# Nine due times of routing matmuls moved in a three-part kernel (linear attention, gated layer, eight routed experts)

## The chip, the cores and the metric

The kernel runs on one core of one Trainium2 chip. The metric is the device time of one execution in microseconds, on the slowest (here the only) core. TensorE is called PE below, VectorE DVE, ScalarE ACT, GpSimd POOL; SP issues DMAs.

## The reference, cut to what matters

Three stages stand one behind the other, on 3072 tokens of width 512. The third is the one that the change touches:

```python
x = linear attention with decay (4 x 8 heads, 768 steps, head size 64)   # -> 3072 x 512
h = x @ w_in;  g = h * tanh(softplus(h));  x = g @ w_out                 # 512 -> 2048 -> 512

def _moe2_ref(x, w_gate, w1, w2):            # E = 8 experts, 1024 wide
    cap = N // E                             # 384 tokens for each expert
    logits = x @ w_gate
    order = np.argsort(-logits.flatten())    # best (token, expert) pairs first
    for idx in order:
        tok, e = idx // E, idx % E
        if assigned[tok] >= 0 or counts[e] >= cap: continue
        assigned[tok] = e; counts[e] += 1
    for e in range(E):
        mask = assigned == e
        out[mask] = np.maximum(x[mask] @ w1[e], 0.0) @ w2[e]
```

Each expert gets exactly 384 tokens.

## The kernel before

All large products are made of three half-precision ones (high by high, high by low, low by high), so each operand is split in a high and a low part. Attention and the gated layer fill the span up to about 780 us. The experts follow one another on PE from 801 us to the end. An expert runs over 8 blocks of its hidden width (12 products of 128x384 each) and then over 3 blocks of its 384 tokens (24 products of 128x512 each), 168 products in all. They are recorded at line 526 in the helper `mm3`, which pauses after every 4 products. Their results go to PSUM buffers `ph` and `px` in turn; ACT (lines 922, 923, 940) and DVE (line 924) empty these.

**Routing** (`route_round`, round r fills one expert) runs beside this, mostly on DVE. A round finds the threshold score of the expert that fills first, by five base-64 digits. For digit i there is a compare on DVE (`against`, line 695, into tile `ld`; the first digit's compare is the largest), then a count on PE (`pc`, 24 small products, line 743), a test on DVE (745), and an answer product on PE (`pn`, line 748) that DVE reads back (750, 754). They are named by round: `pc4x0x` is the first count of round 4 and `pn4x9x` its last answer. After the last answer DVE marks the chosen tokens (lines 759 to 770), PE makes two products for their positions (`pp`, lines 789 and 790), and DVE takes the chosen ones out of the score table `L` (792, 794), from which the next round starts (705 to 726, then the compare of its first digit). `route_list` makes a round's list of token numbers: compares on DVE in three groups into tile `amt` (line 695), 24 small products on PE (`pl`, line 823), and the list is read at 826 and 828. It is needed for gathering the tokens of that expert, on POOL's queue.

**Weights** (`weights`): for each expert the two weight matrices are loaded by an indirect DMA on POOL's queue (line 866) once the round has named the expert (`EWI`, line 777), squared and summed on ACT (line 872, four pieces each), totalled on PE (`pt`, line 186), and split into `WIN` or `WOUT` by ACT (229) and DVE (230), four pieces each. Experts with even r use `WIN`, those with odd r `WOUT`.

**What sets the order.** PE and, in this part, ACT run in the order in which the program issues their work; a scheduler orders DVE and POOL. The order is written by the planner `Weave`: it has a clock `now`, which the main line moves by 0.163 (128x384) or 0.216 (128x512) for each product, in pauses of 4 (the constant `pw`); a side step is put into the order at the first pause at or after its due time, and names the wait until its next step (and a cost, such as 0.65 at each answer product, that moves the clock). So a larger wait in this table does not make an engine sleep: it puts the product further behind in PE's order, behind more expert products, and all later steps of the same chain with it. The waits of the routing come from `KN['rs'][r]`: entries 0, 2, 4, 6, 8 are added to the wait ahead of the five counts, entries 1 to 9 (odd) ahead of the five answers, entry 10 ahead of the `pp` products, entry 11 ahead of the list's `pl` products. Two more rules bind the chains: a list is begun only after the `pp` of its round, and round r only after the list of round r-2. `weights` for expert r waits for the round's last answer to be in the order.

Of the kernel before, what the change touches and what calls it, by code (L numbers as in the profile page):

```python
# [20 lines left out]
B, H, S, D = 4, 8, 768, 64  # L21
DM, DFF, E, F = 512, 2048, 8, 1024
# [14 lines left out]
UNIT = [256.0 ** i for i in reversed(range(len(DIGITS)))]  # L37


KN = dict(ea=1, sc=1, pw=4, le=0.0, hl=['P', 'P'], cs=['V', 'V', 'V', 'V', 'V', 'V', 'V'], cc=['V', 'V', 'V', 'V', 'V', 'V', 'V', 'V', 'V'], lo=['c0', 'g', 'c1', 'm', 'c2', 's', 'wg', 'w0', 'w1', 'w2'], ga=['', 'V'], rs=[[-0.63, 0.3, -1.2, 0.0, 0.24, 0.0, 0.09, 0.0, 0.21, 0.0, 0.0, -4.24], [2.1, 0.09, 2.19, 0.0, 0.58, 0.15, 0.18, 0.15, 0.26, 0.26, 1.46, -0.41], [3.26, 0.0, -0.68, 0.2, 0.33, 0.0, -0.3, 0.0, 0.09, -0.12, 0.3, -3.18], [0.56, 0.0, 0.38, 0.0, 0.15, 0.0, 0.12, -0.11, -0.04, -0.27, 0.03, -3.34], [0.67, 0.0, 0.31, -0.76, 0.89, 0.0, 0.15, -0.22, 0.0, 0.0, -0.16, -4.15], [1.46, -2.35, 0.04, -0.29, 0.13, -2.18, 0.42, -0.4, 0.45, 0.03, 1.16, -4.07], [0.45, 0.54, 0.45, 0.0, 1.18, 0.0, -0.39, -0.55, -0.61, -0.05, 0.45, -3.57], [-0.15, 0.0, -0.75, 0.0, 0.0, 0.0, 0.0, -0.3, 0.0, 0.0, 3.28, -3.01]], fs=[[0.0, 0.0, -3.96, -1.22], [-0.75, 0.0, 1.32, 0.16], [0.0, 0.0, -2.08, 0.13], [0.0, -1.13, 0.71, 0.36], [0.0, 0.0, 0.0, -0.56], [0.38, 0.75, 0.13, 0.04], [0.0, 0.38, 0.2, 0.69], [0.0, -1.5, -0.61, 0.29]], av=[5.75, 5.75, 2.0, 4.0], a2=[1.3, 2.2, 4.3], a1=[0.1, 1.0, 0.85], ao=[3.5, 3.5, 3.35], wv=[8.5, 0.5, 1.0, 4.5], ov=5.0, an=[3.0, 3.15, 3.6], qm=['P0', 'VP', 'VP', 'PH', 'P1', 'VV', 'VP'], vm=['P0', 'VP', 'VP', 'VP', 'VP', 'P0', 'VP'], km=['A', 'H', 0, 0, 0, 0, 0], am=['VP', 'VP', 'VP', 'AV', 'VP', 'AV', 'VP'], ss=['V', 'P', 'P', 'P', 'P', 'P', 'P'], sm=['P', 'V', 'V', 'P', 'E', 'D', 'P'], ym=[0, 0, 0], hm=['VVVP', 'VVAV', 'VVVP', 'VVVP', 'AVVP', 'VVVP', 'VVVP', 'VVVP', 'VVVP'], ci=['PP', 'PP', 'AP', 'PP', 'PP', 'PP', 'VP', 'PP'], co=['AP', 'PP', 'PP', 'PP', 'AP', 'PP', 'PP', 'PP'], wa=[15, 12, 8, -1, 7, 16], cp=[0, 100, 0, 100], np=0, yp=[0, 2000], op=[0, 0, 200, 0, 50, 1000], xp=[0, 0, 0, 0, 0, 0], ld=[0, 1, 2, 3, 4], wj=[4, 4, 4], fw=[13.5, 18.5, 14, 16, 14, 16], qs=1.0, tw=3.0, sw=1.5, po=[[0] * 8] * 4, sl=[0, 0, 0.7], rw=[2.6, 2.5, 1.55, 1.7, 1.7], pn=0.5, lw=11.0, gx=9.0, tk=2.75, st=[16.0, 21.0, 20.0, 23.5], wi=['H', 'A', 0, 0, 2, 0, 0, 0], wo=['H', 'H', 0, 0, 0, 0, 'H', 0], tp=[], gw=5.15, nw=1.0, cw=0, sp=50, ap=1000, wp=None, ip=None)  # L40


class Weave:
# [55 lines left out]
def moe_kernel(ctx, tc, qkv, w_in, w_out, w_gate, w1p, w2p,  # L99
# [64 lines left out]
    def first_loads():  # L164
        for x in KN['lo']:
            if x[0] == 'c':
                load_chunk(0, int(x[1]), 3 if x == 'c0' else 1)
            elif x == 'g':
                SY.dma_start(GQ, c_g)
                SY.dma_start(GV, c_gv)  # L170
            elif x == 'm':
                SY.dma_start(MASK, c_mask)
            elif x == 's':
                SY.dma_start(GS, c_gs)
            elif x == 'wg':
                SY.dma_start(wg_raw, w_gate.rearrange("(k p) e -> p k e", p=128))
            else:
                win_load(int(x[1]))


    def col(name, n=1, dt=F32, bufs=2):
        return wk.tile([128, n], dt, name=name, tag=name, bufs=bufs)

    def total(cols, n, tag="tot", name="pm"):
        p = ps.tile([128, 16], F32, name=name, tag="pm", bufs=1)
        T.matmul(p[:, :n], onesf, cols, start=True, stop=True)
        r = col(tag)
        V.tensor_reduce(r, p[:, :n], axis=AX.X, op=OP.add)
        return r

    def pow2(ss, name, bufs=2, n=1):
        a = col(name + "a", n, I32, bufs=bufs)
        V.tensor_scalar(a, ss.bitcast(I32), 1, 0x7F800000, op0=OP.logical_shift_right, op1=OP.bitwise_and)
        r = wk.tile([128, 2, n], I32, name=name, tag=name, bufs=bufs)
        cc = (189 + 16) << 23
        V.tensor_scalar(r[:, 0], a, -1.0, float(cc), op0=OP.mult, op1=OP.add)
        V.tensor_scalar(r[:, 1], a, float((254 << 23) - cc), None, op0=OP.add)
        rf = r.bitcast(F32)
        return rf[:, 0], rf[:, 1]
# [40 lines left out]
    def to_f32(dst, raw, mode='PP'):  # L240

        lo, hi = words(raw)
        di = dst.bitcast(I32)
        hf = hi.bitcast(F32)
        if mode[0] == "A":
            A.activation(dst, hf, AF.Copy, scale=2.0 ** -112)
        else:
            (V if mode[0] == "V" else P).tensor_scalar(dst, hf, 2.0 ** -112, 1.0, op0=OP.mult, op1=OP.mult)
        (V if mode[1] == "V" else P).tensor_scalar(hf, hf, 0.0, 1.0, op0=OP.mult, op1=OP.mult)
        V.scalar_tensor_tensor(di, di, 3, hi, op0=OP.logical_shift_left, op1=OP.bitwise_or)  # L250
        V.scalar_tensor_tensor(di, lo, 29, di, op0=OP.logical_shift_right, op1=OP.bitwise_or)
# [4 lines left out]
    def norm(zs, ss):  # L256

        p = ps_m([128, 128], F32)
        n = len(zs) * 8
        for i, z in enumerate(zs):  # L260
            zb = z.bitcast(BF).rearrange("p (b d two) -> p b d two", d=128, two=2)[:, :, :, 1]
            for b in range(8):
                T.matmul(p, zb[:, b], zb[:, b], start=i + b == 0, stop=8 * i + b == n - 1)
        t = wk.tile([128, 128], F32, name="tr", tag="tr", bufs=1)
        V.tensor_tensor(t, p, identf, op=OP.mult)
        V.tensor_reduce(ss, t, axis=AX.X, op=OP.add)
# [3 lines left out]
    def win_load(i):  # L270
        q, j = divmod(i, 2)
        raw = GF[i % 5 // 3][:, i % 5 % 3 * 2048:i % 5 % 3 * 2048 + 2048]
        SY.dma_start(raw.bitcast(I32).rearrange("p (k f) -> p k f", k=2),
                     w_in_w.rearrange("(k p) f -> p k f", p=128)[:, 2 * j:2 * j + 2, q * 1024:q * 1024 + 1024])
        WIN_RAW.append(raw)
# [3 lines left out]
    def win_setup(q):  # L279

        zs = [RAW[:, i * 1024:i * 1024 + 1024] for i in (2 * q, 2 * q + 1)]
        for j in range(2):
            with tc.high_priority(offset=KN['cp'][q]):
              to_f32(zs[j], WIN_RAW[2 * q + j], KN['ci'][2 * q + j])
            if 2 * q + j < 3:
                win_load(2 * q + j + 5)
        yield KN['wv'][0], 0.0
        yield KN['wv'][1], 1.0
        ss = col("ssi")
        norm(zs, ss)  # L290
        yield KN['wv'][2], 0.2
        sw = pow2(total(ss, 1, "toti"), "swin", 4)
# [925 lines left out]
```

## Time and profile before

| what | value |
|---|---|
| median of 3 runs | 1115.99 us (1115.18 to 1117.84) |
| the profiled execution | 1116.19 us |
| its span, first to last instruction | 1114.3 us |
| PE busy | 972.5 us, 87% of the span |
| DVE busy | 774.0 us, 69% |
| ACT busy | 648.8 us, 58% |
| POOL busy | 417.6 us, 37% |
| mean granted TensorE clock | 0.94 of full speed |

The last 313 us hold the eight experts. The profile names each small product by its round and step, so that each place of the routing can be found in the trace of PE in order of time.

### The profile page before, as it was taken

How to read it: one execution, taken by the hardware profiler on the slowest of the kernel's cores; microseconds unless marked ns; L12 is line 12 of the kernel's file. 1: busy time of each engine (PE TensorE's matmuls, PEld its weight loads, DVE VectorE, ACT ScalarE, POOL GpSimd, SP SyncE). 2: the span in 40 equal slices, each digit the busy share in tenths (PEclk: the TensorE clock that was granted, in tenths of full speed). 3: DMA queues.
4: the chain of work that ended last, by engine and by line, in shares of the span. 5: the costliest groups of instructions: out<-in, count | busy, mean ns of one | idle time of the engine just before them, and what ended most of it. 6: DMA issues, size and time to landing. Idle time of an engine off the chain costs nothing. (4 is left out here: it accounts for less than half of the span.)

```text
span 1114.3 us, 19615 instructions
## 1 busy us (share of the span) xinstructions
PE 972.5 (87%) x7897; PEld 560.0 (50%) x7897; DVE 774.0 (69%) x1630; ACT 648.8 (58%) x989; POOL 417.6 (37%) x304
## 2 busy tenths in 40 slices
PE   3348758888999999999999989999598898899997
PEld 2335434444655555656556546454354454455553
DVE  6899998954666787677776745568779777754530
ACT  4435856554467577577567567316365763767751
POOL 5956365461432553534554513200222222123211
PEclk9959878969999999999999989999699998999999
DMA  8461262157113113121144010053464465266300
GB/s 307 124 189 39 104 179 58 49 104 152 26 52 85 40 57 77 48 76 39 48 105 92 14 38 1 11 194 119 95 218 171 110 193 189 58 218 225 116 29 29
DMA packets 108811, 113.65 MB, mean 102 GB/s; under 512 B 92464, under 2 KB 92592, under 8 KB 106672
## 3 DMA queue, kind: packets, MB, share of 16 engines
q1 hardware_dynamic: 102576, 66.24, 23.0%
q0 software_dynamic: 6144, 46.15, 11.6%
q8 instruction: 62, 1.02, 0.4%
q14 instruction: 29, 0.24, 0.1%
HBM read 77.50 MB, written 13.64 MB: 82 GB/s over the span
## 5 line engine op out<-in xcount | busy, mean ns | idle before, releaser
L526 PE MATMUL ph<-xt,WIN 128*128 128x384 f16 x1728 | 334.8, 336 | 7.5 <-DVE RAW L556 3.2
L526 PE MATMUL px<-WOUT,G 128*128 128x512 f16 x1248 | 312.7, 385 | 0.2 <-DVE WOUT L230 0.2
L526 PEld LDWEIGHTS <-WIN 128*128 128x128 f16 x1920 | 188.6, 101 | 151.9 <-issue 27.4
L526 PEld LDWEIGHTS <-G 128*128 128x128 f16 x1728 | 164.6, 99 | 173.2 <-issue 9.0
L578 POOL TENSOR_TENSOR G<-RAW,G 128x1536 f16<-128x1536 f32 (+1 forms) x32 | 99.5, 3108 | 104.8 <-DVE G L575 88.8
L407 POOL TENSOR_TENSOR amt<-amt 128x512 f16<-128x512 f32 x40 | 55.7, 1393 | 120.7 <-DVE amt L404 106.0
L556 DVE TENSOR_SCALAR RAW<-ph 128x384 f32<-128x384 f32 x124 | 68.1, 551 | 43.1 <-PE ph L526 42.5
L563 ACT ACTIVATE RAW<-RAW,zt,ch 128x1536 f32<-128x1536 f32 x32 | 53.3, 1664 | 49.1 <-DVE RAW L556 44.0
L326 ACT ACTIVATE junk<-ld 128x512 bf16<-128x512 f32 x63 | 39.4, 626 | 61.1 <-DMA ld<-in_qkv_dram 60.2
L924 DVE TENSOR_TENSOR G<-G,G 128x384 f16<-128x384 f32 x64 | 35.4, 554 | 56.3 <-ACT G L923 56.2
L572 DVE TENSOR_TENSOR RAW<-RAW 128x1536 f32<-128x1536 f32 (+1 forms) x33 | 60.7, 1839 | 15.5 <-ACT RAW L571 15.4
L872 ACT ACTIVATE junk<-RAW 128x1024 bf16<-128x1024 f32 x64 | 67.6, 1056 | 5.4 <-DMA RAW<-in_w1p_dram,MASK 2.9
L224 POOL TENSOR_TENSOR RAW<-ld,RAW 128x512 f16<-128x512 f32 x34 | 45.7, 1358 | 50.9 <-ACT RAW L223 49.2
L941 POOL DMA_INDIRECT out_dram<-G,MASK x18 | 23.4, 1300 | 96.3 <-ACT G L940 94.8
L526 PEld LDWEIGHTS <-WOUT 128*128 128x128 f16 x384 | 37.9, 101 | 26.8 <-issue 4.2
L401 DVE TENSOR_TENSOR amt<-pa,MASK 128x512 f32<-128x512 f32 x38 | 26.1, 688 | 35.5 <-PE pa L400 31.1
L571 ACT ACTIVATE RAW<-RAW 128x1536 f32<-128x1536 f32 (+1 forms) x33 | 47.7, 1446 | 0.4
L224 POOL TENSOR_TENSOR STH<-SC,STH 64x256 f16<-64x256 f32 x34 | 32.0, 942 | 42.0 <-ACT STH L223 38.9
L564 ACT ACTIVATE RAW<-RAW 128x1536 f32<-128x1536 f32 x32 | 47.2, 1475 | 0.3
L526 PE MATMUL ph<-WOUT,G 128*128 128x512 f16 x192 | 44.5, 379 | 0.5 <-DVE G L924 0.4
L695 DVE TENSOR_TENSOR ld<-MASK,ld 128x1536 bf16<-128x1536 bf16 (+1 forms) x35 | 44.6, 1274 | 0.5
L526 PE MATMUL px<-WIN,G 128*128 128x512 f16 x192 | 44.1, 380 | 0.0
(571 smaller groups left out, 1946.2 us busy)
## 6 DMA issues: line engine op xcount, KB each, us to landing
ld<-in_qkv_dram SPq DMA_DIRECT2D x20, 768.0 KB, 4.7
G<-in_w_in_dram SPq DMA_DIRECT2D x8, 1024.0 KB, 7.1
G<-in_w_out_dram SPq DMA_DIRECT2D x8, 1024.0 KB, 5.9
x_rows<-xr SPq DMA_DIRECT2D x24, 256.5 KB, 3.1
G<-in_qkv_dram SPq DMA_DIRECT2D x2, 768.0 KB, 6.7
g_columns<-G SPq DMA_DIRECT2D x1, 1024.0 KB, 8.4
G<-g_columns SPq DMA_DIRECT2D x1, 1024.0 KB, 7.3
ld<-in_qkv_dram SPq DMA_DIRECT2D x3, 256.0 KB, 2.9
```

Of the source, the lines that this page charges most:

```text
L224: (V if pool in ("V", "E") else P).tensor_tensor(lo, src, hi, op=OP.subtract)
L326: A.activation(junk(), x.rearrange("p a d -> p (a d)"), AF.Square, accum_out=ss[:, i:i + 1])
L407: (P if mode[1] == "P" else V).tensor_tensor(amh[:, j, 1], am, amh[:, j, 0], op=OP.subtract)
L526: T.matmul(p, a, b, start=i == 0, stop=i == n - 1)
L556: V.tensor_scalar(hs[:, f], p[:, :G], 1.0 / 65536.0, None, op0=OP.mult)
L563: A.activation(th, hs, AF.Tanh, scale=ch[:, q:q + 1], bias=z)
L564: A.activation(th, th, AF.Arctan, scale=-0.5, bias=0.5)
L571: A.activation(th[:, w], th[:, w], AF.Sin, scale=-2.0, bias=math.pi / 2)
L572: (V if hm[1] == 'V' else P).tensor_tensor(th[:, w], th[:, w], hs[:, w], op=OP.mult)
L578: (P if lo == 'P' else V).tensor_tensor(gb[:, 1, o], th[:, w], gb[:, 0, o], op=OP.subtract)
L695: V.tensor_tensor(out.rearrange("p t (j v) -> p t j v", v=VR), cv[:, ts, None, :].to_broadcast([128, n, J // VR, VR]), RT["jr"][:, i, :J]. ...
L872: A.activation(junk(1024), RAW[:, o:o + 1024], AF.Square, accum_out=ss[:, j:j + 1])
```

## The change

Only the table `rs` of the planner's constants differs. No instruction is added or removed; nine waits get other values (rounds count from 0):

```diff
 rs, entry:        first count (0)   positions (10)   list (11)
-round 2                                              -3.18
+round 2                                              -1.68
-round 3                              0.03            -3.34
+round 3                              2.73            -2.54
-round 4            0.67             -0.16
+round 4           -0.53              3.34
-round 5            1.46              1.16            -4.07
+round 5           -1.04              3.66            -2.07
-round 6                              0.45
+round 6                              2.95
```

So the `pp` products of rounds 3, 4, 5 and 6 are due 2.7, 3.5, 2.5 and 2.5 later, the `pl` products of lists 2, 3 and 5 are due 1.5, 0.8 and 2.0 later (counted from the place where their chain stands), and the first counts of rounds 4 and 5 are due 1.2 and 2.5 sooner.

## Rows read from the trace of the kernel before

**Rows 1.** Busy time by expert (1, 2, 3, 7): stretch, length, engines' busy, clock, DMA
```profile
841.46:882.98 41.52, 37.29 (x348) 21.17 (x347) 33.15 (x90) 25.91 (x44) 10.35 (x8) 1.00 0.50 159
882.98:929.59 46.61, 39.80 (x327) 21.98 (x326) 37.41 (x102) 29.80 (x47) 12.08 (x9) 0.92 0.47 142
929.59:977.11 47.52, 40.90 (x324) 21.85 (x323) 34.96 (x95) 25.86 (x43) 9.47 (x10) 0.90 0.46 148
1074.97:1106.27 31.30, 31.30 (x169) 16.35 (x167) 4.46 (x8) 9.05 (x19) 2.91 (x3) 1.00 0.07 26
```

**Rows 2.** PE's waits from 801.3 to 1107 us: waiter, awaited, us, times, longest
```profile
PE pp4x10x L789 <- DVE MASK L765: 3.2, 1, 3.2
PE pp3x10x L789 <- DVE MASK L765: 2.2, 1, 2.2
PE pp5x10x L789 <- DVE MASK L765: 2.1, 1, 2.1
PE pp6x10x L789 <- DVE MASK L765: 2.0, 1, 2.0
PE pc6x0x L743 <- DVE MASK L726: 1.5, 1, 1.5
PE pt5x3x L186 <- DVE se L196: 1.4, 1, 1.4
PE pl2x11x L823 <- DVE amt L695: 1.1, 2, 0.8
...
PE pl5x11x L823 <- DVE amt L695: 1.0, 2, 0.7
...
PE pl5x11x L823 <- DVE GQ L816: 0.8, 1, 0.8
...
PE pc6x8x L743 <- DVE ld L695: 0.8, 1, 0.8
PE pl3x11x L823 <- DVE amt L695: 0.7, 1, 0.7
...
PE pp6x10x L790 <- DVE MASK L770: 0.3, 1, 0.3
```

**Rows 3.** PE in order of time behind `pp` of round 4: start, us, instructions
```profile
889.64 2.73 PE L526 MATMUL ph<-xt,WIN 128*128 128x384 f16 x8
892.17 3.59 PE L526 MATMUL px<-xt,WIN 128*128 128x384 f16 x12
895.59 2.11 PE L526 MATMUL ph<-xt,WIN 128*128 128x384 f16 x12
897.54 2.11 PE L526 MATMUL px<-xt,WIN 128*128 128x384 f16 x12
```

**Rows 4.** PE in order of time behind `pp` of round 5 and behind `pl` of list 5
```profile
928.59 1.21 PE L526 MATMUL px<-WIN,G 128*128 128x512 f16 x4
...
933.08 2.11 PE L526 MATMUL px<-xt,WOUT 128*128 128x384 f16 x12
...
942.12 2.72 PE L526 MATMUL px<-xt,WOUT 128*128 128x384 f16 x8
...
948.10 1.46 PE L526 MATMUL px<-xt,WOUT 128*128 128x384 f16 x8
```

**Rows 5.** DVE in order of time: from `pp` to the next round's first compare
```profile
852.28 0.21 DVE L792 SCALAR_TENSOR_TENSOR MASK<-pp3x10x,MASK 128x48 f32<-128x48 f32 x1
...
854.97 1.75 DVE L695 TENSOR_TENSOR ld<-MASK,ld 128x3072 bf16<-128x3072 bf16 x1
...
890.38 1.28 DVE L230 SCALAR_TENSOR_TENSOR WOUT<-RAW,se,WOUT 128x1024 f16<-128x1024 f32 x1
...
893.89 1.75 DVE L695 TENSOR_TENSOR ld<-MASK,ld 128x3072 bf16<-128x3072 bf16 x1
...
937.57 0.35 DVE L726 TENSOR_TENSOR MASK<-MASK 128x192 bf16<-128x192 f32 x1
```

**Rows 6.** DMA issues from 760 to 1114 us: size or count, median us to landing
```profile
RAW<-in_w1p_dram,MASK POOLq DMA_INDIRECT x7, 9.7
```

## What the change will do: the prediction

> **What bounds the kernel now.** The page gives PE as the busiest engine, and the last 305 us are where the moved products stand. So I cut the last 305 us by expert [rows 1]. Expert 7, which has no routing beside it, takes 31.30 us at full clock, and PE is busy all of it: this is the floor of an expert. Experts 1, 2 and 3 take 41.52, 46.61 and 47.52 us. Part of the excess is the routing's own products, which stay. The rest is PE idle or PE slow: in expert 2 it is busy 39.80 of 46.61 us at a mean granted clock of 0.92, in expert 3 40.90 of 47.52 us at 0.90. DVE is the busiest other engine (37.41 us in expert 2), but it is not full. From 801 us to the end PE runs one fixed order with the same products before and after, so a wait there is paid by everything behind it: the end moves by what PE's waits and slow stretches change.
>
> Then PE's waits, by name [rows 2]. The four longest are the `pp` products of rounds 4, 3, 5 and 6, each for DVE's marking of the chosen tokens: 3.2, 2.2, 2.1 and 2.0 us. After each of them the second `pp` product waits again for the running sum, 0.2 to 0.3 us (four such, the longest is shown). The lists 2, 5 and 3 cost 1.1, 1.0 + 0.8 and 0.7. So these products stand too early in PE's order: PE reaches them and nothing behind them may pass.
>
> Last, what follows a wait. Behind `pp` of round 4 [rows 3] 8 + 12 products take 895.59 - 889.64 = 5.95 us; the next 12 take 897.54 - 895.59 = 1.95, that is 0.1625 each, so 20 should take 3.25. The loss is 2.70: PE was granted the lower of its two clock levels, 1.2 in place of 2.4 GHz. Behind `pp` of round 5 [rows 4] 4 wide and 12 narrow products take 4.49 us instead of 2.8 (a wide one is (31.30 - 96 x 0.1625)/72 = 0.218 by expert 7), a loss of 1.7. Behind list 5 24 narrow products and an answer take 948.10 - 942.12 = 5.98 instead of 3.9 to 4.0, a loss of 2.0. Together 6.4 us of slow clock.
>
> **The change part by part.** The planner's table moves products in PE's order; I added up its due times by hand for both tables (4 expert products move its clock by 0.65 or 0.86, a step lands at the first pause at or after its due time). Number of expert products between two steps, before and after:
>
> - last answer to `pp`: round 3 16 to 32, round 4 12 to 36, round 5 16 to 36, round 6 12 to 32
> - `pp` to the next round's first count: 3 to 4 40 to 32, 4 to 5 44 to 28, 5 to 6 36 to 36
> - first count to list: list 2 4 to 12, list 3 4 to 16, list 5 4 to 20; list 4 stays 44 behind its `pp`
> - from there on the rounds stand later by 8 (round 4), 16 to 20 (round 5), 28 to 36 (round 6) and 52 products (the `pp` of round 7)
> - the w1 loads of experts 4, 5, 6, 7 move 4, 8, 20, 24 products later with their first squares; their w2 loads move by 4 or less
>
> *The `pp` products.* What PE needs between the last answer and `pp` is its work there plus its wait. Round 3: 16 x 0.1625 + 2.2 + 0.2 = 5.0; now it has 32 x 0.1625 = 5.2. Round 4: 12 x 0.1625 + 3.2 + 0.2 = 5.4; now 5.85. Round 5: 2.8 + 2.1 + 0.2 = 5.1; now about 6.1. Round 6: 12 x 0.218 + 2.0 + 0.3 = 4.9; now 5.2 (narrow products stand there then). All four are covered if DVE takes as long as before. Gone: 3.2 + 2.2 + 2.1 + 2.0 + 0.9 = 10.4; what is left of it I bound by 0 and 1.5 and take 0.4.
>
> *The lists.* Lists 2 and 5 get 8 and 16 more products in front (1.3 and 2.6 us or more) against waits of 1.1 and 1.8; list 3 gets 4 more behind its `pp` (0.65) against 0.7. Gone 3.6. But the answer product of the next round now stands ahead of the list and needs DVE while DVE is in the list's compares: one such piece is worth 0.7 by the wait of list 3. I put 0 to 0.7 at three places and take 0.9 in all.
>
> *First counts, sooner.* After `pp` DVE needs up to the end of the first compare: round 3 to 4 856.72 - 852.28 = 4.4 us; round 4 to 5 893.89 + 1.75 - 889.64 = 6.0 us, since a split of 1.28 and an emptying stand between; round 5 to 6 937.92 - 928.59 = 9.3 us [rows 3 to 5]. PE now has 5.2, 4.55 and 5.85. So the count of round 4 waits 0 to 0.8, that of round 5 0 to 1.5, that of round 6 0 to 3.5, where it waits 1.5 now. I take 0, 0.7 and 0.3, near the row of round 3 to 4, since the splits that stretched the other two are due 36 to 44 products ahead of the new `pp` places. The 1.5 of today counts as gone.
>
> *What comes along.* The fifth count of round 6 (0.8) and the total of w2 of expert 5 (1.4) wait behind splits and squares. The splits of expert 5 now end 16 products ahead of that count, and the squares of w1 of expert 6 no longer alternate with those of w2 of expert 5. Gone 2.2 at best; I keep half, 1.1.
>
> *Loads.* A w1 load needs 9.7 us [rows 6]. Its first square stands 80 to 88 products behind its due place (13 to 14 us), but the index comes from DVE after the last answer, as late as `pp` does, some 5 us. So ACT, which also empties PSUM and works in order, may stand 0 to 2 us at two of the loads: 1.0 taken. The experts' starts are far off: the splits of w1 for experts 6 and 7 end more than 150 products before these begin. Moving them and the lists costs nothing by that cover.
>
> *Clock.* 6.4 us go if nothing falls any more. I keep 1.7, one fall such as that of round 5. The trace says that waits alone do not decide it: after the 2.2 of round 3 the clock stayed (expert 1 has 1.00 [rows 1]), after the 2.1 of round 5 it fell. The Trainium skill, "TensorE: Matmul & The Clock Gate", section "A second HAM failure mode: psum-queue depth-cycling", says that short idles between groups, if frequent, suffice for the clock to swing. The fall behind list 5, after pieces of 0.7 and 0.8 and the 1.5 of a count, agrees with it.
>
> Sum: waits gone 10.4 + 3.6 + 1.5 + 2.2 = 17.7, clock 6.4, together 24.1. Given back 0.4 + 0.9 + 1.0 + 1.1 + 1.0 + 1.7 = 6.1. Gain 18.0 from 1116.19 of the profiled execution: **1098**. The median shown is 0.2 lower, which changes nothing. The last scatter hangs on PE's last product as before.
>
> **The rivals.**
> - *The waits move to the next product.* DVE's chain is a fixed length, and what PE no longer waits for at `pp` it waits for at the first count. For it: the 6.0 and 9.3 us that DVE took behind rounds 4 and 5 [rows 3 to 5]. Against: the splits are due earlier relative to it. Price: counts 0.8 + 1.5 + 3.5 and 0.7 at three places, and two of three falls stay (4.7): 24.1 - 0.4 - 5.8 - 2.1 - 1.0 - 1.1 - 4.7 = 9.0, so 1107.
> - *Clock falls all the same.* Waits vanish as summed, but the short ones left keep the three falls: 18.0 - 4.7 = 13.3, so 1103. The section named above would give this. Against: at most five waits under 1 us are left.
> - *Slower: loads late.* ACT holds the experts' evictions behind squares whose weights have not landed; PE fills both PSUM pairs and stands. It decides only if five loads (w1 of experts 3 to 7) each land so late that PE stands more than 18.0/5 = 3.6 us at each; at the full 9.7 us of a load it would be 5 x 9.7 - 18.0 = 30 slower, 1147. Against: the first squares stand 13 to 14 us of products behind the loads, and a load takes 9.7 us.
> - *No effect.* It would need the new due times to be swallowed by the rule that a round waits for the list two rounds back. They are not: list 3 stands 120 products ahead of the place where round 5 starts, list 4 104 ahead of that of round 6; only an error in my adding would give 1116.
>
> **How the numbers follow.** Forecast case (gain 14 to 24) 0.67, clock 0.13, waits moved 0.12, slower 0.04, no effect 0.04. The range reaches from 1091 (all 24.1 and one more short wait) to 1108, which takes in the first two rivals; about 0.1 is left above and 0.1 below or between. A measurement can tell about 0.2%, 2.2 us. Faster 0.92, same 0.04, slower 0.04.
>
> **What would show it.** Right: no `pp` among PE's waits over 0.5 us, experts 1 to 3 at about 39 us each, a clock of 0.97 or more in experts 2 and 3, counts of rounds 5 and 6 waiting under 1 us. Wrong: waits of 1.5 us or more at the first counts (waits moved), a clock under 0.95 with short waits (clock), ACT idle for a weight load with PE idle beside it (loads).

## The result and the profile after

| kernel | median, us | range, us | runs |
|---|---|---|---|
| before | 1116.16 | 1113.86 to 1117.84 | 6 |
| after | 1107.34 | 1103.26 to 1108.27 | 6 |

The ratio is 0.9916, 95% interval 0.9896 to 0.9936: faster by 0.84%, or 8.8 us. The forecast was 18.0 us, so half of the gain came. The profiled execution of after took 1108.27 us with a span of 1106.5; its span is 7.8 shorter than that of before (1114.3). All that follows is measured on these two spans and accounts for 7.8.

First the stretches of the experts, cut at the first product of each, as in [rows 1]. The columns are the same: stretch, length, busy time of PE, of PE's weight loads, of DVE, ACT and POOL, then the granted clock, the DMA share and GB/s. Experts 1, 2 and 3 of after:

```profile
841.34:888.85 47.51, 41.62 (x324) 21.85 (x323) 35.67 (x90) 28.11 (x45) 10.04 (x9) 0.89 0.44 139
888.85:932.72 43.87, 40.33 (x349) 22.31 (x348) 31.36 (x89) 25.84 (x43) 7.21 (x7) 0.92 0.50 144
932.72:971.50 38.78, 36.26 (x323) 20.39 (x322) 34.10 (x87) 28.06 (x46) 11.22 (x9) 1.00 0.55 177
```

Expert 3 went from 47.52 to 38.78 at full clock, as forecast. Expert 2 went from 46.61 to 43.87 only. Expert 1, which ran at a granted clock of 1.00 before, runs at 0.89 now and is 6.0 us **longer**. With the smaller changes (first product 0.53 later, expert 0 shorter by 0.65, expert 4 by 1.35, expert 5 by 0.9) the sum is 0.5 - 0.65 + 6.0 - 2.7 - 8.7 - 1.35 - 0.9 = -7.8, the whole difference of the spans. The 0.53 at the start stems from a gather of token rows ahead of expert 0, on which PE waits 3.1 us in after and 2.0 in before; over the runs below that wait lies anywhere between 0.3 and 3.6, without following what was moved, so I do not count it to the change. (That it belongs to the single execution is not shown.)

PE's waits of after from 790 to 1100 us (waiter, line, awaited, total, times, longest), which answer to [rows 2]:

```profile
...
PE pl3x11x L823 <- DVE amt L695: 2.4, 1, 2.4
PE pc4x6x L743 <- DVE ld L695: 2.3, 1, 2.3
PE pl4x11x L823 <- DVE amt L695: 1.8, 1, 1.8
...
PE pc6x8x L743 <- DVE ld L695: 1.7, 1, 1.7
...
PE pc5x0x L743 <- DVE MASK L726: 1.3, 1, 1.3
...
PE pc6x0x L743 <- DVE ld L695: 0.7, 1, 0.7
...
PE pl5x11x L823 <- DVE amt L695: 0.2, 1, 0.2
```

No `pp` product is left among them. But, the gather of expert 0 and round 2 aside, four new or larger waits stand at the head: lists 3 and 4, the fourth count of round 4 (`pc4x6`) and the first count of round 5. Summed over all of PE's rows behind the start of expert 0, waits fell from 20.5 to 12.7 us, by 7.8; the forecast was 17.7 - 0.4 - 0.9 - 1.0 - 1.1 = 14.3.

PE in order of time through experts 1 and 2 of after (start, us, instruction, products; in brackets the wait ahead of it):

```profile
859.42 0.17 PE L748 MATMUL pn4x1x<-MASK,onesb 128*128 128x8 bf16 x1
860.96 0.77 PE L823 MATMUL pl3x11x<-GQ,amt 128*128 128x6 bf16 x16
864.11 0.35 PE L823 MATMUL pl3x11x<-GQ,amt 128*128 128x6 bf16 x8 [2.38 <-DVE amt L695]
864.33 4.44 PE L526 MATMUL ph<-WOUT,G 128*128 128x512 f16 x12
868.60 0.75 PE L743 MATMUL pc4x2x<-MASK,ld 128*128 128x8 bf16 x24
...
881.34 0.79 PE L743 MATMUL pc4x6x<-MASK,ld 128*128 128x8 bf16 x24 [2.28 <-DVE ld L695]
...
882.42 3.57 PE L526 MATMUL ph<-WOUT,G 128*128 128x512 f16 x8
885.93 0.18 PE L748 MATMUL pn4x7x<-MASK,onesb 64*128 64x8 bf16 x1
886.04 2.97 PE L526 MATMUL ph<-WOUT,G 128*128 128x512 f16 x8
888.85 1.46 PE L526 MATMUL px<-xt,WIN 128*128 128x384 f16 x8
...
906.42 3.26 PE L526 MATMUL ph<-xt,WIN 128*128 128x384 f16 x12
909.51 0.55 PE L823 MATMUL pl4x11x<-GQ,amt 128*128 128x6 bf16 x16
911.83 0.35 PE L823 MATMUL pl4x11x<-GQ,amt 128*128 128x6 bf16 x8 [1.78 <-DVE amt L695]
```

Behind list 3, 12 wide products take 868.60 - 864.33 = 4.27 us instead of 12 x 0.218 = 2.6: 1.7 lost to the clock. Behind `pc4x6`, 8 take 885.93 - 882.42 = 3.51 and 8 take 888.85 - 886.04 = 2.81, each instead of 1.74: 2.8 lost. Between the first count of round 5 and list 4, 12 narrow products take 909.51 - 906.42 = 3.09 instead of 1.95, and 0.5 is lost just ahead of them: 1.7. Behind list 4 another 1.3 goes. Added up in this way from expert 1 on, the slow clock cost 6.4 us in before (the prediction's sum) and 7.5 in after. So the clock gave nothing back: the falls behind `pp` went, and others took their place.

That places expert 1: 2.4 + 1.7 + 2.3 + 2.8 = 9.2 us now, against `pp` of round 3 (2.2 and 0.2) and the list 3 of before (0.7), 3.1 together, where the clock had not fallen at all. The difference of 6.1 is, to 0.1, the measured 6.0.

Why list 3 waits more although it stands 48 expert products behind its `pp` instead of 44 is seen on DVE. First DVE of before, then of after, around the list's three compares (`amt`, 0.68 each) and the large compare of round 4's next digit (`ld`, 1.75):

```profile
858.39 0.68 DVE L695 TENSOR_TENSOR amt<-GQ,ld 128x1024 bf16<-128x1024 bf16 x1
...
859.21 0.68 DVE L695 TENSOR_TENSOR amt<-GQ,ld 128x1024 bf16<-128x1024 bf16 x1
...
860.35 0.68 DVE L695 TENSOR_TENSOR amt<-GQ,ld 128x1024 bf16<-128x1024 bf16 x1
...
862.84 1.76 DVE L695 TENSOR_TENSOR ld<-MASK,ld 128x3072 bf16<-128x3072 bf16 x1
```

```profile
859.41 0.68 DVE L695 TENSOR_TENSOR amt<-GQ,ld 128x1024 bf16<-128x1024 bf16 x1
860.01 0.16 DVE L750 TENSOR_REDUCE MASK<-pn4x1x 128x1 f32<-128x8 f32 x1
...
860.63 0.68 DVE L695 TENSOR_TENSOR amt<-GQ,ld 128x1024 bf16<-128x1024 bf16 x1
861.24 0.55 DVE L924 TENSOR_TENSOR G<-G,G 128x384 f16<-128x384 f32 x1
861.71 1.75 DVE L695 TENSOR_TENSOR ld<-MASK,ld 128x3072 bf16<-128x3072 bf16 x1
863.37 0.68 DVE L695 TENSOR_TENSOR amt<-GQ,ld 128x1024 bf16<-128x1024 bf16 x1
```

In before the answer `pn4x1` stood behind the list in PE's order, so DVE could only make round 4's compare after the list's third. In after the answer stands 8 expert products ahead of the list, and DVE's fixed order takes the answer (860.01) and the large compare (861.71) before the list's third. From DVE's step behind `pp` (L792) to the end of that third compare it is 8.75 us in before (852.28 to 861.03, the first in [rows 5]) and 11.4 in after (852.64 to 864.05). In round 4 the same span grew from 11.0 to 13.3: there the answer `pn5x1` stood directly ahead of list 4 in before, and DVE made the list first all the same; in after it stands 16 products ahead, and the large compare comes between.

The wait at `pc4x6` is seen on DVE of after, too: three splits of expert 2's w2 (line 230) come between the test of the count before it (`pc4x4`) and the compare that `pc4x6` needs, which ends at 881.28:

```profile
874.33 0.16 DVE L745 TENSOR_SCALAR MASK<-pc4x4x 64x8 bf16<-64x8 f32 x1 [2.42 <-PE pc4x4x L743]
...
876.30 1.28 DVE L230 SCALAR_TENSOR_TENSOR WIN<-RAW,se,WIN 128x1024 f16<-128x1024 f32 x1 [0.41 <-ACT WIN L229]
...
879.13 1.28 DVE L230 SCALAR_TENSOR_TENSOR WIN<-RAW,se,WIN 128x1024 f16<-128x1024 f32 x1
880.33 0.95 DVE L695 TENSOR_TENSOR ld<-MASK,ld 128x1536 bf16<-128x1536 bf16 x1
```

In before DVE made that compare at 874.07, ahead of all of them.

### The profile page after: what moved, and what is told of

Read it like the earlier page. It is cut to its first block, busy times and chain, and to the rows that moved or that the text cites. A ratio compares the mean times of both kernels' runs of the same rounds, so it can differ in the third digit from the quotient of the medians.

```text
span 1106.5 us, 19618 instructions
## 1 busy us (share of the span) xinstructions
PE 968.8 (88%) x7897; PEld 558.7 (50%) x7897; DVE 772.9 (70%) x1630; ACT 649.0 (59%) x989; POOL 413.5 (37%) x304
## 5 line engine op out<-in xcount | busy, mean ns | idle before, releaser
L224 POOL TENSOR_TENSOR RAW<-ld,RAW 128x512 f16<-128x512 f32 x34 | 45.6, 1357 | 50.7 <-ACT RAW L223 49.0
L526 PE MATMUL ph<-WOUT,G 128*128 128x512 f16 x192 | 48.7, 407 | 0.0
L571 ACT ACTIVATE RAW<-RAW 128x1536 f32<-128x1536 f32 (+1 forms) x33 | 47.7, 1445 | 0.4
L230 DVE SCALAR_TENSOR_TENSOR WOUT<-RAW,se,WOUT 128x1024 f16<-128x1024 f32 x32 | 40.4, 1278 | 7.1 <-ACT WOUT L229 7.0
```

What stands on the lines that cost most here:

```text
L224: (V if pool in ("V", "E") else P).tensor_tensor(lo, src, hi, op=OP.subtract)
L230: V.scalar_tensor_tensor(lo, src, s, hi, op0=OP.mult, op1=OP.subtract)
L526: T.matmul(p, a, b, start=i == 0, stop=i == n - 1)
L571: A.activation(th[:, w], th[:, w], AF.Sin, scale=-2.0, bias=math.pi / 2)
```

## The experiments

The theory (A in the quoted texts): the gain was lost where an answer now stands some products ahead of a list, since DVE then makes the next digit's compare between the list's compares; and where round 4, moved by 8 products, meets the splits of expert 2's w2 on DVE (`pc4x6`). Its rivals, under other letters, say that the lists stand at the wrong distance, that the sooner first counts by themselves or the clock are at fault, or that the `pp` moves bring less than was summed. A number in brackets behind `rs` is round and entry: 10 the positions, 11 the list, 0 the first count. All medians, in us, with the ratio to before measured beside it; the length of experts 1, 2, 3 and 5 comes from the profile of each. Expert 4 takes 33 to 36 us in all of them but three (four `pp` alone, first counts back, four `pp` and list 2), where it takes 37 to 37.5.

| kernel | median | ratio [95%] | experts 1, 2, 3 and 5 |
|---|---|---|---|
| before | 1116.2 | | 41.5, 46.6, 47.5, 32.3 |
| after | 1107.3 | 0.9916 [0.9896, 0.9936] | 47.5, 43.9, 38.8, 31.4 |
| four `pp` alone | 1101.2 | 0.9868 [0.9838, 0.9898] | 38.5, 43.2, 38.6, 31.4 |
| the other five alone | 1123.6 | 1.0069 [1.0052, 1.0087] | 44.2, 47.7, 45.3, 38.9 |
| lists 3, 4 later | 1101.0 | 0.9852 [0.9825, 0.9879] | 43.6, 43.3, 38.9, 31.4 |
| list 3 sooner | 1105.5 | 0.9898 [0.9870, 0.9927] | 44.2, 45.9, 38.9, 31.4 |
| first counts back | 1105.7 | 0.9894 [0.9876, 0.9912] | 41.5, 43.6, 40.3, 31.4 |
| lists back | 1112.2 | 0.9970 [0.9951, 0.9988] | 49.3, 43.9, 43.1, 31.4 |
| lists later, splits later | 1105.4 | 0.9906 [0.9869, 0.9942] | 37.7, 45.0, 41.7, 35.8 |
| `pp` of round 4 alone | 1122.7 | 1.0063 [1.0043, 1.0084] | 43.1, 44.6, 48.8, 38.8 |
| list's compares first on DVE | 1104.9 | 0.9910 [0.9882, 0.9939] | 44.6, 45.0, 40.0, 31.4 |
| round 3 as before | 1108.4 | 0.9934 [0.9915, 0.9953] | 41.5, 45.6, 37.0, 39.8 |
| four `pp` and list 2 | 1098.5 | 0.9826 [0.9785, 0.9868] | 38.5, 39.6, 40.6, 31.4 |
| whole list first on DVE | 1099.8 | 0.9860 [0.9835, 0.9885] | 41.8, 43.1, 38.1, 31.4 |

**The four `pp` moves alone.** Before, with

```diff
-rs[3][10] = 0.03; rs[4][10] = -0.16; rs[5][10] = 1.16; rs[6][10] = 0.45
+rs[3][10] = 2.73; rs[4][10] = 3.34; rs[5][10] = 3.66; rs[6][10] = 2.95
```

> The kernel before with only the four later position products (rounds 3 to 6); lists 2, 3, 5 and the first counts keep their old waits. Theory A (what the change gained at the position products it gave back at lists 3 and 4, where the answer product now stands ahead of the list and DVE makes the next digit's large compare before the list's third group, and at the third digit of round 4, which slid behind the splits of w2 of expert 2): no position product waits over 0.5 us, lists 3 and 4 stand ahead of the next answer as before and wait under 1 us, the count pc4x6 waits 2 us or more with a fall of the clock; 1106 us, plus or minus 3. Theory B (my sum as forecast): 10.4 us of waits and about 5 us of clock go and little comes back, 1100 us. Theory C (DVE is the bound, every wait removed turns up elsewhere): within 3 us of before, 1113 to 1116 us.

Measured 1101.2, ratio 0.9868 [0.9838, 0.9898]: 15 us by themselves, where the whole change gives 8.8. That is the number of theory B, my sum, and not A's 1106; of the 15.8 by which the profiled span is shorter, 2.1 lie ahead of expert 0, where nothing was moved. PE's waits of this kernel:

```profile
PE pn5x5x L748 <- DVE MASK L745: 1.9, 1, 1.9
PE pc6x8x L743 <- DVE ld L695: 1.9, 1, 1.9
...
PE pl3x11x L823 <- DVE amt L695: 0.5, 2, 0.3
```

No `pp`, no wait at list 4, three pieces of 0.3 at list 3, and no `pc4x6`: that it would wait was expected and did not happen. Without the sooner first counts round 4 stands 16 products later than in before and not 8, so that 24 products stand between the total from which the splits start (`pt2x3`) and `pc4x6` in place of 20, and DVE makes two splits ahead of the compare in place of three. The answers stand as in before (behind list 3, directly ahead of list 4), DVE makes the lists first, and it needs 8.7 us in round 3 and 9.1 in round 4 from L792 to the end of the list's third compare. The slow clock cost about 3 us from expert 1 on, against 6.4 in before and 7.5 in after.

**The other five alone.** Before, with lists 2, 3 and 5 later and the two first counts sooner, `pp` where it was:

```diff
-rs[2][11] = -3.18; rs[3][11] = -3.34; rs[5][11] = -4.07; rs[4][0] = 0.67; rs[5][0] = 1.46
+rs[2][11] = -1.68; rs[3][11] = -2.54; rs[5][11] = -2.07; rs[4][0] = -0.53; rs[5][0] = -1.04
```

> The other half alone: the kernel before with the later lists 2, 3, 5 and the sooner first counts of rounds 4 and 5, the position products of rounds 3 to 6 due as before. Theory A: the four position products still wait 2 to 3 us each, the first count of round 5 comes 28 expert products behind its positions and waits about 1.3 us, lists gain 1 to 2 us: 1112 to 1118 us. Theory B: the same, since the sum puts 1 to 3 us on these parts. Theory C: 1116 us.

Measured 1123.6, slower by 0.7% and worse than every theory had it. `pp` of rounds 3 and 4 wait 2.2 and 3.1 as before; list 5 waits 4.6 for its inputs (L816) and 1.7 for its compares, list 4 1.8; and PE stands 5.1 at the totals of expert 7's w1 (`pt7x2`), of which more below. So half of the change is a loss. 15 faster and 7.5 slower make 7.4, near the 8.8 measured, but by way of other waits: after has neither the 5.1 at `pt7x2` nor the 4.6 at list 5.

**Lists 3 and 4 later still.** After, with

```diff
-rs[3][11] = -2.54; rs[4][11] = -4.15
+rs[3][11] = 0.06; rs[4][11] = -2.15
```

> The changed kernel with lists 3 and 4 due 2.6 and 2.0 later (12 and 8 expert products), nothing else moved in PE's order. Theory A: the waits of 2.4 and 1.8 us at these lists go to under 0.5 us and the slow clock behind them (1.7 and about 1.3 us) goes with them: 5 to 8 us faster than the changed kernel, 1100 to 1102 us. Theory C: the waits turn up at the next counts, under 2 us faster.

Measured 1101.0, ratio 0.9852 [0.9825, 0.9879]. Neither list waits any more. `pc4x6` waits 3.6 in place of 2.3: PE reaches it sooner by what the list gave back, and DVE has it no sooner. Of the 2.4 + 1.8 and the falls behind them (1.7 + 1.3) 6.3 us are won, by the medians, as A has it.

**List 3 sooner.** After, with

```diff
-rs[3][11] = -2.54
+rs[3][11] = -4.5
```

> The changed kernel with list 3 due 2.0 sooner, so that it stands ahead of the first answer of round 4 again, 12 expert products (about 2.2 us) earlier. Theory A (the wait comes from DVE's order, which follows that of PE): DVE makes the list's third group ahead of the next digit's compare again, and the list waits about 1.5 us, less than the 2.4 of the changed kernel although it stands earlier; 1 to 3 us faster than the changed kernel. Rival D (the list is simply too early by a fixed DVE time): it waits 2.4 + 2.2 = 4.6 us; 1 to 3 us slower than the changed kernel.

The list now stands ahead of the answer again. It waits 1.4 for its inputs and 0.5 for its compares, 1.9 in place of 2.4, although it stands sooner. A had 1.5 and the rival, by which only the distance from `pp` counts, 4.6. The time, 1105.5, is not told apart from after.

**First counts back.** After, with

```diff
-rs[4][0] = -0.53; rs[5][0] = -1.04
+rs[4][0] = 0.67; rs[5][0] = 1.46
```

> The changed kernel with the first counts of rounds 4 and 5 due as before (the position products and lists 2, 3, 5 stay later). Theory A (the sooner counts put the answers of rounds 4 and 5 ahead of lists 3 and 4, and DVE then makes the next large compare ahead of the list's third group): list 4 stands level with the count again and waits under 1 us, 1100 to 1103 us, close to the position products alone. Rival E (the later lists cost): 1106 to 1109 us, as the changed kernel.

1105.7 lies between the two forecasts and decides nothing by its time. The list waits are gone, as A says: both answers stand directly ahead of their lists, too late for DVE to make the large compare first. Expert 1 is back at 41.5. But answers and late counts of rounds 4 to 6 wait about 2 us each (`pn4x3` 2.0, `pn5x5` 1.9, `pc6x8` 2.2). Why they do so here, while the four `pp` moves alone, with lists sooner, have fewer of them, was not settled. One comparison goes against the later lists: four `pp` and list 2 (the last run below) differs from this kernel in lists 3 and 5 alone, which are later here, and takes 1098.5 (its interval ends at 0.9868, this one begins at 0.9876). The cause of that difference is open: 2.9 us of it lie in expert 0, where PE's order is the same in both.

**Lists back.** After, with lists 2, 3 and 5 as before:

```diff
-rs[2][11] = -1.68; rs[3][11] = -2.54; rs[5][11] = -2.07
+rs[2][11] = -3.18; rs[3][11] = -3.34; rs[5][11] = -4.07
```

> The changed kernel with lists 2, 3 and 5 due as before (the position products later and the first counts sooner stay). Theory A: lists 3 and 4 still stand behind the answers of rounds 4 and 5, list 3 four products nearer, and wait 2 to 3 us each; list 2 waits 1 us again: 1106 to 1110 us. Rival E: 1100 to 1103 us.

1112.2, above both forecasts (A 1106 to 1110) and clearly slower than after. List 3 waits 3.2, list 4 1.8, list 2 1.0 and list 5 1.4. The rival, that moving the lists was the mistake, would have given 1100 to 1103 and falls here: with the sooner first counts later lists are right, and what was wrong is what was put ahead of them. That does not hold without the sooner counts, where the run before stands beside four `pp` and list 2.

**Lists later and the splits too.** The kernel with lists 3 and 4 later, and the splits of expert 2's w2 due 1.3 later, so that round 4's compare for `pc4x6` comes ahead of them on DVE:

```diff
-fs[2][3] = 0.13
+fs[2][3] = 1.43
```

> Lists 3 and 4 due later as in the run before of that name, and the total of w2 of expert 2 (with the four splits that follow it) due 1.3 later, level with the third answer of round 4 as in the kernel before. Theory A: the count pc4x6 (3.6 us there, with 1.8 us of slow clock behind it) stops waiting, 4 to 5 us less than 1101: 1096 to 1098 us. Rival C (DVE is full in that stretch, a wait taken away turns up at the next count): pc4x6 and pc4x8 together wait 3 us or more, 1100 to 1102 us.

```profile
PE pc5x0x L743 <- DVE ld L695: 2.5, 1, 2.5
PE pt7x2x L186 <- ACT junk L872: 2.2, 1, 2.2
PE pn5x5x L748 <- DVE MASK L745: 1.9, 1, 1.9
PE pc6x6x L743 <- DVE ld L695: 1.9, 1, 1.9
```

The wait at `pc4x6` is gone and expert 1 falls from 43.6 to 37.7, the shortest of all runs. A is right in that place: it was DVE in the splits, and DVE makes the compare ahead of them here (870.45 us). But it is wrong in the sum, as is C (1100 to 1102): the totals of later loads moved too, from 4 products sooner to 20 later, and PE waits in rounds 5 and 6 and at expert 7's w1 instead (rows above). Experts 2, 3 and 5 give back 1.6 + 2.8 + 4.3, and 1105.4 is 4 us worse than without the step by the medians; the intervals of the two ratios just touch.

**`pp` of round 4 alone.** Before, with

```diff
-rs[4][10] = -0.16
+rs[4][10] = 3.34
```

> The kernel before with the position products of round 4 alone due later (24 expert products behind their old place). Theory A and my sum: the wait of 3.2 + 0.2 us and the slow clock of 2.7 us behind it go, and since the first count of round 5 and list 4 keep their distances nothing comes back at once: 5 to 6 us less than before, 1110 to 1111 us. Rival C: the gain turns up as other waits, 1114 to 1116 us.

The largest single wait of before, 3.2 + 0.2 with 2.7 of slow clock behind it, was expected to bring 5 to 6. The kernel is 0.6% **slower**, 1122.7. PE behind the moved `pp`:

```profile
895.65 0.76 PE L743 MATMUL pc5x0x<-MASK,ld 128*128 128x8 bf16 x24
896.94 0.17 PE L748 MATMUL pn5x1x<-MASK,onesb 128*128 128x8 bf16 x1 [0.53 <-DVE MASK L745]
898.77 0.34 PE L823 MATMUL pl4x11x<-GQ,amt 128*128 128x6 bf16 x8 [1.67 <-DVE GQ L816]
901.04 0.37 PE L823 MATMUL pl4x11x<-GQ,amt 128*128 128x6 bf16 x8 [1.94 <-DVE amt L695]
901.65 0.38 PE L823 MATMUL pl4x11x<-GQ,amt 128*128 128x6 bf16 x8 [0.23 <-DVE amt L695]
901.88 4.00 PE L526 MATMUL ph<-xt,WIN 128*128 128x384 f16 x12
```

PE is through with the 44 products behind `pp` at full clock, and DVE is not: 12.6 us pass from its L792 to the end of list 4's last compare (889.00 to 901.59), with the large compare of round 5 in between. (The answer stands directly ahead of the list here, as in before; what makes DVE's scheduler put the list first there and not here is open.) In before it was 11.0, and PE's 44 products took 44 x 0.1625 + 2.7 = 9.85 instead of 7.15 [rows 3], and PE waited little: **the slow clock had covered the list.** So 0.5 + 1.7 + 2.2 came back in waits, and behind them the clock fell again (901.88: 12 products in 3.80 instead of 1.95). DVE's longer chain has its part in this: in the four `pp` moves together it needs 9.1 in this place, and PE, with the same 44 products at full clock, waits only 1.1. Here nothing of the gain is left behind the list: this kernel is ahead of before by 1.7 us at `pn4x9` (882.06 against 883.73) and by 1.2 at `pt4x2` (917.76 against 918.92). Expert 2 is 2.0 shorter only because `pp` of round 5 (2.1 + 0.2 of wait in before) now stands 16 products behind its end.

The loss itself is far off, for the most part in expert 5, which is 6.5 longer: PE waits 4.5 at `pt7x2` for ACT's squares, and ACT for the w1 load of expert 7:

```profile
1023.59 1.06 ACT L872 ACTIVATE junk<-RAW 128x1024 bf16<-128x1024 f32 x1 [3.73 <-DMA RAW<-in_w1p_dram,MASK]
```

In before ACT waits for no weight load between 800 and 1075 us.

**Round 3 as before.** After, with the three entries of round 3's `pp`, list 3 and round 4's first count undone:

```diff
-rs[3][10] = 2.73; rs[3][11] = -2.54; rs[4][0] = -0.53
+rs[3][10] = 0.03; rs[3][11] = -3.34; rs[4][0] = 0.67
```

> The changed kernel with round 3's positions, list 3 and the first count of round 4 due as before; all that belongs to rounds 4 to 6 keeps its own new waits. Theory A: expert 1 falls back to about 41.5 us (47.5 in the changed kernel), with the position product of round 3 waiting 2.2 us again, pc4x6 not waiting; experts 2 and 3 keep their gain: 3 to 6 us less than the changed kernel, 1101 to 1104 us. If the gain in experts 2 and 3 hung on round 3 being late, 1108 to 1114 us.

Expert 1 is back at 41.5, as expected: list 3 waits 0.7 as in before, `pc4x6` not at all. Experts 2 and 3 together keep their gain (82.6 us, 82.7 in after). But the whole takes 1108.4, in the range set for the case that this gain is lost, and for another reason. First PE, then ACT, in expert 5:

```profile
1021.03 0.59 PE L186 MATMUL pt7x2x<-sse,onesf 128*128 128x4 f32 x2 [5.55 <-ACT junk L872]
```

```profile
1011.52 1.06 ACT L872 ACTIVATE junk<-RAW 128x1024 bf16<-128x1024 f32 x1 [3.41 <-DMA RAW<-in_w1p_dram,MASK]
```

Expert 5 is 8.4 longer than in after; without that the kernel would stand near 1100. This is the prediction's "loads late", at one load instead of five, and not for a late index: DVE had expert 7's index at 965.7 us here (line 784), and the w1 load was issued at 999.3. It was issued 1.3 us behind the w2 load of expert 6 and landed after 12.2 us; in before it was issued 1.3 us ahead of that load and landed after 8.9. That the order of the two makes the difference is not shown by a run of its own. The same wait of PE carries 5.1 of the loss of the other five alone and 4.5 of that of round 4's `pp` alone. After itself escapes it: there ACT waits 1.9 in all for w1 loads and `pt7x2` not at all.

**The list's compares first on DVE.** After, with nothing moved on PE; DVE's scheduler is told to prefer the three compares of a list, in every round:

```diff
-            against(oh[:, t:t + 8], pjv, OP.is_equal, len(DIGITS) - 1, slice(t, t + 8))
+            with tc.high_priority(): against(oh[:, t:t + 8], pjv, OP.is_equal, len(DIGITS) - 1, slice(t, t + 8))
```

> The changed kernel with one priority more: the three groups of a list's compares on DVE come ahead of the next answer's read-back and of the next digit's compare. The order of PE, ACT, POOL and SP is the changed kernel's; only DVE's differs. Theory A (lists 3 and 4 wait because DVE makes the 1.7 us compare between the list's second and third group): lists 3 and 4 wait under 0.5 us each and the slow clock right behind list 3 (1.7 us) goes: 4 to 7 us less than the changed kernel, 1100 to 1103 us. Theory C (DVE is full there, its order does not matter): the answers or counts behind wait by as much, within 2 us of the changed kernel, 1105 to 1109 us.

```profile
PE pl3x11x L823 <- DVE GQ L816: 3.0, 1, 3.0
```

A miss of the edit: the compares come early, but the list's other input (`mv`, L816) is now the one behind the large compare, and list 3 waits 3.0 for that. List 4 no longer waits, but the answer `pn5x1` ahead of it now does (1.9), as C had it. 1104.9 is not told apart from after.

**The whole list first on DVE.** The same, with the lines of `em` (L813) and `mv` (L816) preferred too:

```diff
-        V.tensor_tensor(em, pj[:, 1, :, None].to_broadcast([128, NT, CPG]),
+        with tc.high_priority(): V.tensor_tensor(em, pj[:, 1, :, None].to_broadcast([128, NT, CPG]),
...
-        V.tensor_tensor(mv, em[:, :, :, None].to_broadcast([128, NT, CPG, 2]),
+        with tc.high_priority(): V.tensor_tensor(mv, em[:, :, :, None].to_broadcast([128, NT, CPG, 2]),
```

> As the run groups_first, with the list's two small steps on DVE that its groups do not need but its product does (lines 813 and 816) also ahead of the next digit's compare. PE, ACT, POOL and SP keep the changed kernel's order. Theory A (what list 3 waits for is whatever part of the list DVE makes behind the 1.7 us compare: the third group in the changed kernel, line 816 in groups_first): list 3 waits under 1 us (2.4 and 3.0 in those two), expert 1 takes 44 us or less (47.5 and 44.6), 1101 to 1104 us. Theory C: list 3's wait goes over to the next count or answer, expert 1 stays at 44.5 us or more, 1104 to 1107 us.

```profile
859.72 1.89 DVE L695 TENSOR_TENSOR amt<-GQ,ld 128x1024 bf16<-128x1024 bf16 x3
861.52 0.30 DVE L816 TENSOR_TENSOR GQ<-GQ,ld 128x144 bf16<-128x144 bf16 x1
...
863.20 1.76 DVE L695 TENSOR_TENSOR ld<-MASK,ld 128x3072 bf16<-128x3072 bf16 x1
```

```profile
PE pc4x6x L743 <- DVE ld L695: 2.3, 1, 2.3
PE pn5x1x L748 <- DVE MASK L745: 2.2, 1, 2.2
```

DVE makes the list's three compares and `mv` together and the large compare behind them, 8.4 us after L792 instead of 11.4. List 3 waits no more, expert 1 is 41.8 instead of 47.5, and the kernel takes 1099.8, ratio 0.9860 [0.9835, 0.9885]: some 6 us faster than after by its ratio, with PE's order untouched, and a little below what A had forecast. This settles the first half of A for list 3: the order on DVE alone was worth those 6 us, nearly all in expert 1. At list 4 C is right: its wait of 1.8 went over to `pn5x1` (2.2), and expert 2 is only 0.8 shorter. The second half of A, `pc4x6`, still waits 2.3, as it should.

**Four `pp` and list 2.** The four `pp` moves alone, and list 2 as in after:

```diff
-rs[2][11] = -3.18
+rs[2][11] = -1.68
```

> The position products alone, as in the run of that name, and list 2 due 1.5 later as in the change. List 2 stands in expert 0, with nothing else moved near it: its waits of 0.8 and 0.2 us go: about 1 us less than 1101, 1099 to 1101 us. If the time saved there turns up again as a wait behind it, 1101 to 1104 us.

1098.5, ratio 0.9826 [0.9785, 0.9868]: the lowest median of all, better than both kernels. By the intervals it is not told apart from the four `pp` moves alone, from lists 3 and 4 later, or from the whole list first on DVE. Expert 0 is 1.0 shorter, as expected of list 2; the other 1.7 of the medians are not placed. What is left are seven waits of 0.9 to 1.9 on counts and answers. The time is that forecast for the whole change, reached with five of its nine parts.

## Why the prediction was half right

The time lies in the range, and the sign was right; the sum was not, and the range held because it had been drawn wide enough to take in the first two rivals. Of 18.0 forecast 7.8 came, 10.2 less: waits 6.5 less (7.8 of 14.3), clock 5.8 less (-1.1 of 4.7), the start 0.5, against 1.0 set aside for loads that were not late. That adds to 11.8; the 1.6 beyond are gains in pieces too small for the rows I summed, and I did not place them.

- *The `pp` products.* Right: none of the four, nor of the second products behind them, is left among PE's waits. The four moves alone gave 15.
- *The lists.* Lists 2 and 5 fell to 0.3 or less, as forecast. The failed step is "one such piece is worth 0.7 by the wait of list 3 ... take 0.9 in all", together with "list 4 stays 44 behind its `pp`" at no cost. I priced an answer ahead of a list as a small wait of PE. Its price is the compare that DVE makes once the answer is there: 1.75 with its small steps, 2.7 in all in round 3 (8.75 to 11.4). Lists 3 and 4 waited 2.4 + 1.8, with 1.7 + 1.3 of clock behind them. Undoing that order on DVE alone gave some 6 us back, nearly all of it at list 3.
- *List 4's cover.* Its 44 products were the same in number and not in time. I counted the 2.7 of slow clock behind `pp` as pure gain, while DVE used them. `pp` of round 4 alone shows it: of a gain of 6.1 by the prediction's terms (3.4 + 2.7) nothing was left behind list 4.
- *First counts.* Within their bounds, and 2.2 in all against 1.0 taken: round 4 0.2 (took 0), round 5 1.3 (took 0.7, bound 1.5), round 6 0.7 (took 0.3).
- *What isn't in the sum.* `pc4x6`: 2.3 of wait and 2.8 of clock. The prediction says that round 4 stands 8 products later, and it follows the splits only against `pp` and against the experts that use them, not against round 4's own middle counts. The splits stayed, the count did not, and DVE was in them.
- *What comes along.* `pt5x3` is gone (1.4); `pc6x8` rose from 0.8 to 1.7: 0.5 net, against the 1.1 kept.
- *Clock.* 1.7 was kept and 7.5 stayed. The forecast of "at most five waits under 1 us" failed, and with it the ground on which falls were struck out. The Trainium skill's rule that the prediction weighs ("TensorE: Matmul & The Clock Gate", "A second HAM failure mode: psum-queue depth-cycling") says that the clock may swing with short idles between groups if they are frequent; here each fall of after from expert 1 on stands behind a single wait of 1.3 to 2.4 us. That fits the rule loosely: the rows of after show no fall from frequent short idles alone, and no size of a wait from which the clock falls (below).
- *The rivals.* Two came together: waits moved to the next product (though to lists and middle counts more than to the first counts on which I set the price) and the clock fell all the same. The first had 1107, which is the measured time, by other terms. "Loads late" did not happen in after, but it is a real mechanism at expert 7's w1, as four of the runs show; I had the right engine (ACT in order behind a load), but PE stands at the total of the squares and not at full PSUM buffers, the index is not what is late, and I priced it over five loads, where one is enough for 4 to 8 us.

What stays open: which of the small waits of rounds 5 and 6 (`pn5x5`, `pc6x8`, about 2 us each in most kernels) follow from which move; why expert 7's w1 load lands late in some of the kernels and not in others; and what decides whether a wait is followed by a fall.

## What to carry to other kernels

A wait on an in-order engine is the end of another engine's chain: before a product is moved, follow that chain to its next consumer as well, and count the distance in time at full speed, since a slow stretch behind a wait may be what hides the next one. If a move changes the order of two consumers, look at what the supplier's scheduler will then put between them; it cost more here than the wait itself. And parts of such a table are tried one by one and in groups: the largest wait taken alone made this kernel slower, four of them together took 15 us off, and all nine parts 9.

## What the runs showed of the hardware that was not expected

The granted clock does not follow the length of the last wait alone. It fell behind waits of 2.38 (1.7 us lost), 2.28 (2.8), 1.78 (1.3) and 1.26 us (1.7) in after and behind 3.2 in before, and it did not fall behind 2.2 (`pp` of round 3) and 2.0 (`pp` of round 6) in before, nor behind 1.7 (`pc6x8`) in after, where expert 3 has 1.00 throughout. Nor is it the same in two kernels at the same place: up to `pp` of round 3 PE's order in `pp` of round 4 alone is that of before, the wait there is 2.2 us in both, and the clock fell behind it there (1.6 us lost) and not in before.

ACT's longest wait for a w1 load went from nothing in before to 1.7 us in after and, at expert 7's load, to 2.3, 3.3, 3.4 and 3.7 in the four kernels in which PE then waits at `pt7x2` (2.2, 5.1, 5.6 and 4.5). Moves of products in PE's order did this (routing products alone, but for one of the four kernels, in which a total and its splits moved too); no transfer was added or made larger. The four `pp` moves alone have two such waits of ACT too, up to 1.9, and PE does not wait for them.
